# Window attention and a two-layer MLP in split f32: where split weights live, which engine takes the rests, and from which chunk seven products are used

## The chip, the cores and the metric

One NeuronCore of one Trainium2 chip; the other cores are idle. The metric is the device time of one execution in microseconds, median of several runs. A core has five engines with instruction queues of their own: PE (TensorE, matrix products), ACT (ScalarE), DVE (VectorE), POOL (GpSimd) and SP (SyncE, which here issues the DMAs). Each runs its instructions strictly in its order and waits on semaphores where an operand or a room isn't ready.

## The reference

Attention in windows, then a two-layer MLP; everything is f32, and the tokens of all batches are the rows of the MLP.

```python
def _attn_ref(q, k, v):                       # 8 batches, 8 heads, 576 positions, 64 wide
    scores = scale * np.matmul(q, k.transpose(0, 1, 3, 2))
    mask_plain = (rel >= 0) & (rel < window)                                  # window 32
    mask_dil = (rel >= 0) & (rel < window * dilation) & (rel % dilation == 0)  # dilation 4
    masks = [mask_plain if h < H // 2 else mask_dil for h in range(H)]
    scores = np.where(masks, scores, -1000000000.0)
    attn = np.exp(scores - max); attn = attn / (sum(attn) + 1e-09)
    return np.matmul(attn, v)
def _moe_ref(x, w_in, w_out):                 # x 4608 x 512, w_in 512 x 2048, w_out 2048 x 512
    h = x @ w_in
    g = np.where(h > 0.0, h, np.exp(np.minimum(h, 0.0)) - 1.0)
    return (g @ w_out)
```

## The kernel before

**Chunks.** The MLP's 4608 tokens go in nine chunks of 512 (`TC`). In a chunk the hidden width is 16 blocks `f` of 128 (`NF`). `gemm1` makes the block h (128 hidden by 512 tokens), `elu` makes g of it (ACT exp and relu, one DVE instruction, L555 or L557), and `second_product` adds g times w_out into four output banks. GEMM2 of f comes two blocks after GEMM1 of f (`LAG = 2`).

**Split operands.** A product at full f32 accuracy costs PE a doubled pass per product, so operands are split: a high part, rounded to the format PE takes at full pace (ACT, a copy), and a rest, operand minus high part, made by one subtraction (DVE). A product is then three: high·high, high·rest, rest·high. The names are `wh`/`wl` for weights (`split_w`, L180, L181), `xh`/`xl` for tokens (`split_x`, L522), `gh`/`gl` for g (L563, L564). In chunk 0 the first blocks are done before anything is split, with plain f32 products: GEMM1 for f < 7 (`F1`), GEMM2 for f < 11 (`F2`).

**Chunk 0 also turns the weights to f32.** They arrive as 64-bit words (512 KB for a block of 128 x 512). They are taken in 16 pairs k = 0..15, in order of need: pair k holds w_in of block k+1 and w_out of block k−1 (pair 0 holds w_in of 0 and 1, pair 15 w_out of 14 and 15). For each pair ACT takes the magnitude of the upper word (`magnitude`, L129) and DVE makes the f32 bits with four instructions (`convert`): two TENSOR_SCALAR (L137, L139) and two SCALAR_TENSOR_TENSOR (L147, L149). From k = 4 on, two pairs go in one set of 2048 wide instructions. The rooms: raw words in `r0` to `r3` (two pairs each, used in turn), f32 in `a0` to `a7`. In chunk 0 and 1 the split weights take rooms that have come free; the table `LATE` lists where.

**Attention.** Batch 0 runs ahead of the MLP (`first_attention`, and the loads of pairs 1 to 3 come behind its maxima, L112, L115). Batch 1 runs within chunk 0 (`second_attention`): E makes scores, masks, maxima and exponentials; X normalises and transposes on DVE; O multiplies by v. Its exponentials are 12 small ACT instructions that also sum. Later batches run beside later chunks.

**Plain and combined chunks.** Chunks 0 to 2 (`CS = 3`) do GEMM1 block by block. From chunk 3 on it is done in groups of four blocks with seven products of half size in place of eight (`combined_chunk`). These need sums of weight blocks, split again (`combine`: f32 blocks, kept in DRAM by `keep_whole`, come back; four adds, two casts, two rests; stores into the DRAM scratch `combined`). Eight of these are done, three in chunk 1 and five in chunk 2 (`COMBINE`). In a combined chunk the weights come from the scratch through four rooms of `r0`.

**What sets the order.** A scheduler places instructions of each engine by priority; `keep_in_program_order` and `issue_after(x)` tie an instruction to an earlier one of the same engine only. SP takes its DMA issues in one queue.

Of the kernel before, what the change touches and what calls it, by code (L numbers as in the profile page):

```python
# [35 lines left out]
NR = NF // 4  # L36
NE = 2
LAG = 2
F1 = 7
F2 = 11  # L40
# [3 lines left out]
CS = 3  # L44
# [10 lines left out]
WHEN = {1: (0, 6, 7, 13), 2: (1, 6, 7, 12)}  # L55
# [3 lines left out]
PLAIN = ("a5", "a-1'")  # L59
COMBINE = {(1, 11): 0, (1, 13): 1, (1, 15): 2, (2, 1): 3, (2, 4): 4, (2, 6): 5, (2, 9): 6, (2, 11): 7}  # L60
# [6 lines left out]
def body(ctx: ExitStack, tc: tile.TileContext, q, k, v, masks, w_in, w_out, out):  # L67
# [19 lines left out]

    early2 = [wst.tile([P, 2, 4 * DM], F32, name=f"r{NR - NE + i}") for i in range(NE)]
    early = [early2[i // 2][:, i % 2, :] for i in range(2 * NE)]
# [3 lines left out]
    raw2, raw, full4, full2, full = [None] * (NF // 2), [None] * NF, [None] * (NF // 2), [None] * NF, [None] * 2 * NF  # L93
# [12 lines left out]
    def load_w(k, behind=None):  # L106

        if k % 2 == 0:
            raw2[k // 2] = wst.tile([P, 4, DM], I64, name=f"r{k // 2 % NR}")
        raw[k] = raw2[k // 2][:, k % 2 * 2:k % 2 * 2 + 2, :]  # L110
        if behind is not None:
            nc.gpsimd.tensor_copy(out=raw[k].bitcast(F32)[:QB, :, 0:1], in_=behind[:, 0:2].unsqueeze(2))  # L112
        for t in range(2):
            i = need[2 * k + t]
            nc.sync.dma_start(out=raw[k][:, t, :], in_=(w_in, w_out)[i % 2][i // 2])  # L115

    def words(j):

        u = raw2[j].rearrange("p t c -> p (t c)").bitcast(U32).rearrange("p (c two) -> p c two", two=2)
        return u[:, :, 0], u[:, :, 1]  # L120

    def magnitude(k):
        j, part = k // 2, slice(k % 2 * 2 * DM, (k % 2 + 1) * 2 * DM)
        if k % 2 == 0:
            full4[j] = wst.tile([P, 4, DM], F32, name=f"a{j}")
        full2[k] = full4[j][:, k % 2 * 2:k % 2 * 2 + 2, :]
        for t in range(2):
            full[need[2 * k + t]] = full2[k][:, t, :]
        return nc.scalar.activation(out=full4[j].rearrange("p t c -> p (t c)")[:, part], in_=words(j)[1][:, part].bitcast(F32), func=AF.Abs)  # L129

    def convert(j, keep=lambda ins: ins, part=slice(0, 4 * DM), behind=None):

        lo, hi = [u[:, part] for u in words(j)]
        a = full4[j].rearrange("p t c -> p (t c)")[:, part]
        au = a.bitcast(U32)

        keep(nc.vector.tensor_scalar(out=a, in0=a, scalar1=TINY, scalar2=None, op0=ALU.max))  # L137

        keep(nc.vector.tensor_scalar(out=au, in0=au, scalar1=0x07FFFFFF, scalar2=3, op0=ALU.bitwise_and, op1=ALU.logical_shift_left))  # L139
# [12 lines left out]
    taken = {}  # L152

    def room_of(name):

        if name not in taken:
            taken[name] = wst.tile([P, 4 if name[0] == "a" else 8, DM], F32 if name in PLAIN else F32R, name=name[:3].rstrip("'"))
        return taken[name]

    def slots(name, *at):  # L160

        step = at[1] - at[0] if len(at) > 1 else 1
        return room_of(name)[:, at[0]:at[-1] + 1:step, :]
# [12 lines left out]
    def split_w(k, t0, t1, places=None):

        h, l = places or places_of(k, t0, t1)
        w = full2[k][:, t0:t1, :]
        nc.scalar.copy(out=h, in_=w)  # L180
        nc.vector.tensor_tensor(out=l, in0=w, in1=h.bitcast(F32), op=ALU.subtract)  # L181
        for t in range(t0, t1):
            wh[need[2 * k + t]], wl[need[2 * k + t]] = h[:, t - t0, :], l[:, t - t0, :]

    LATE = {0: (("r3", 0, 1), ("r3", 2, 3)), 1: (("r3", 4, 5), ("r3", 6, 7)), 2: (("a7", 0, 1), ("a7", 2, 3)),
# [22 lines left out]
    whole = [tc.dram_tile([P, 2, DM], F32, name=f"whole{p}") for p in range(NF // 2)]  # L208

    def keep_whole(k):  # L210

        for t in range(2):
            i = need[2 * k + t]
            if i % 2 == 0:
                nc.sync.dma_start(out=whole[i // 4][:, i // 2 % 2, :], in_=full[i])

    def combine(p):

        o = p % 2 * 2
# [17 lines left out]
    last_transpose = [None] * B  # L237
# [122 lines left out]
    def exponential(u, sm, nmx, sums):  # L360
        nc.scalar.activation(out=sm[:, u, :], in_=sm[:, u, :], func=AF.Exp, bias=nmx[:, u:u + 1], scale=0.125, accum_out=sums[:, u:u + 1])

# [10 lines left out]
    def exponentials(b, hp, places, sm=None):  # L373
# [8 lines left out]
        nc.vector.tensor_reduce(out=nmx, in_=sm, op=ALU.max, axis=mybir.AxisListType.X)  # L382
        if b == 1:

            maxima.append(nc.vector.tensor_scalar(out=nmx, in0=nmx, scalar1=-0.125, scalar2=None, op0=ALU.mult).ins)
            for u in range(NU):
                exponential(u, sm, nmx, sums)
        else:
            nc.vector.tensor_tensor(out=sm, in0=sm, in1=nmx.unsqueeze(2).broadcast_to([QB, 2 * NU, 2 * G]), op=ALU.subtract)
            nc.scalar.activation(out=sm, in_=sm, func=AF.Exp, scale=0.125)  # L390
            nc.vector.tensor_reduce(out=sums, in_=sm, op=ALU.add, axis=mybir.AxisListType.X)
        return b, hp, sm, nmx, sums

    def probabilities(b, hp, sm, nmx, sums):

        if b == 1:

            for u in range(NU, 2 * NU):
                exponential(u, sm, nmx, sums)
        normalise(nc.vector, sm, sums, lambda ins: ins)  # L400
        tr = transposed()
        for c in range(GU):
            for r in range(2):
                ks, cs, rs = slice((c + r) * G, (c + r + 1) * G), slice(c * G, (c + 1) * G), slice(r * G, (r + 1) * G)
                last_transpose[b] = nc.vector.transpose(out=tr[ks, :, cs], in_=sm[cs, :, rs]).ins
# [24 lines left out]
    def later_probabilities(b, hps, groups):  # L430

        other_sm = slots("a5", 2, 3).rearrange("p o t -> p (o t)")[:QB, :2 * NU * 2 * G].rearrange("p (u j) -> p u j", u=2 * NU)
# [78 lines left out]
    def split_x(c):  # L511
        for hp in range(NC):
# [3 lines left out]
            while t0 < (c + 1) * TC:  # L516
# [5 lines left out]
                last = nc.vector.tensor_tensor(out=xl[hp][:, u], in0=src, in1=xh[hp][:, u].bitcast(F32), op=ALU.subtract)  # L522
# [21 lines left out]
    def elu(h_ps, c, f, v=nc.vector, a=nc.scalar):  # L544
# [16 lines left out]
        gh = slots("r3", 4)[:, 0, :] if (c, f) == (CS - 1, NF - 1) else fp.tile([P, TC], F32R, name="gh", bufs=3)  # L561
        gl = slots("r3", 6)[:, 0, :] if (c, f) == (CS - 1, NF - 2) else slots("a7", 0)[:, 0, :] if (c, f) == (CS - 1, NF - 1) else fp.tile([P, TC], F32R, name="gl", bufs=2)
        high.append(a.copy(out=gh, in_=e).ins)  # L563
        low.append(v.tensor_tensor(out=gl, in0=e, in1=gh.bitcast(F32), op=ALU.subtract).ins)  # L564
# [71 lines left out]
    def take_places():  # L636

        pairs = [tuple(halved(slots(r, o)) for o in at) for r, at in (("a0", (0, 2)), ("a1", (0, 2)), ("r3", (0, 1)))]
# [3 lines left out]
        rows.extend((slots("a-1'", 0, 1), slots("a-1'", 2, 3), slots("a5", 0, 1)))  # L642
        sets.extend(((slots("r1", 0, 1), slots("r1", 2, 3)), (slots("r3", 2, 3), slots("r2", 0, 1)), (slots("a7", 0, 2), slots("a6", 0, 2))))
# [326 lines left out]
```

## Time and profile before

| | us |
|---|---|
| time, median of 3 runs (lowest to highest) | 893.19 (892.83 to 894.97) |
| the profiled execution: time | 892.59 |
| the profiled execution: span in the trace | 890.7 |
| mean granted clock of PE | 0.99 |

The page shows one execution. "busy" is the time in which an engine had an instruction under way; PE's is partly modelled, and a product that waits for its operand can look longer. "x" is a count of instructions, "out<-in" the program's names of tiles, and "<-" behind an idle time what ended it. In the views by stretches, each row has a stretch, its length, busy times of PE, PEld (weight loads), DVE, ACT and POOL, the granted clock, the DMA share and GB/s. In timelines, the first two numbers are start and length.

### The profile page before, as it was taken

The numbers are of one execution on the slowest core, as the hardware profiler recorded it, in microseconds if no ns is written. First come the engines' busy times: TensorE is split into PE (matmuls) and PEld (weight loads), VectorE is DVE, ScalarE is ACT, GpSimd is POOL, SyncE is SP. The second block draws the span as 40 slices with busy tenths as digits, with TensorE's granted clock in tenths as the row PEclk, the third lists the DMA queues.
The fourth block names the chain that finished last, engine by engine and source line by source line (L and its number), as shares of the span: only waits on it lengthen the run. The fifth ranks groups of instructions, "written<-read, shape, count | busy, mean of one in ns | idle before, by whom it ended". The sixth has DMA issues, their size and how long they took to land. (4 is left out here: it accounts for less than half of the span.)

```text
span 890.7 us, 17847 instructions
## 1 busy us (share of the span) xinstructions
PE 866.9 (97%) x7424; PEld 728.4 (82%) x7424; DVE 610.1 (68%) x921; ACT 458.6 (51%) x783; POOL 6.0 (1%) x12
## 2 busy tenths in 40 slices
PE   6999998999989999999999999999999999999998
PEld 4545676887878888898989998989899999998996
DVE  6999996958578878874977487748775533353332
ACT  3665665745655564544554454545554453454334
POOL 2000000000000000000000000000000000000000
PEclk8999998999999999999999999999999999999999
DMA  9996334321463556867576577666765566567541
GB/s 345 380 353 244 118 102 142 109 91 67 160 223 114 192 176 197 255 191 222 179 252 212 182 221 226 220 199 221 212 186 160 175 206 186 171 182 221 185 142 48
DMA packets 66961, 170.68 MB, mean 192 GB/s; under 512 B 6752, under 2 KB 21440, under 8 KB 66880
## 3 DMA queue, kind: packets, MB, share of 16 engines
q1 hardware_dynamic: 66880, 169.54, 59.2%
q8 instruction: 59, 0.97, 0.4%
q14 instruction: 22, 0.18, 0.1%
HBM read 141.20 MB, written 28.31 MB: 190 GB/s over the span
## 5 line engine op out<-in xcount | busy, mean ns | idle before, releaser
L104 PE MATMUL h<-xh,r 128*128 128x256 f32 (+1 forms) x984 | 225.3, 311 | 8.3 <-ACT r L180 3.7
L104 PEld LDWEIGHTS h<-xh,r 128*128 128x128 f32 x984 | 166.2, 192 | 19.9 <-ACT r L180 4.2
L104 PE MATMUL h<-xl,r 128*128 128x256 f32 (+1 forms) x492 | 143.6, 309 | 0.6 <-DVE xl L418 0.6
L104 PE MATMUL o_ps<-a,r 128*128 128x512 f32 x480 | 117.0, 391 | 0.0
L418 DVE SCALAR_TENSOR_TENSOR a-1_3251<-a-1_3251,a 128x1024 f32<-128x1024 f32 x48 | 58.7, 1223 | 83.2 <-ACT a L418 83.0
L418 DVE TENSOR_TENSOR a-1_3251<-h,e 128x512 f32<-128x512 f32 x72 | 49.7, 690 | 82.5 <-PE h L104 82.1
L104 PEld LDWEIGHTS h<-xl,r 128*128 128x128 f32 x492 | 94.4, 192 | 10.4 <-issue 3.5
L104 PEld LDWEIGHTS o_ps<-a,r 128*128 128x128 f32 x480 | 87.6, 188 | 16.5
L104 PE MATMUL o_ps<-a,gh 128*128 128x512 f32 x248 | 89.3, 463 | 0.0
L418 ACT COPY e<-h 128x512 f32<-128x512 f32 x72 | 42.2, 586 | 79.2 <-PE h L104 64.8
L104 PE MATMUL h<-a,r 128*128 128x256 f32 x576 | 77.5, 284 | 0.0
L104 PEld LDWEIGHTS h<-a,r 128*128 128x128 f32 x576 | 74.0, 191 | 3.0
L418 ACT COPY a-1_3251<-h 128x512 f32<-128x512 f32 x24 | 14.1, 587 | 109.6 <-PE h L104 109.6
L104 PEld LDWEIGHTS o_ps<-a,gh 128*128 128x128 f32 x248 | 46.3, 188 | 24.2 <-issue 17.2
L418 ACT ACTIVATE a<-a 128x1024 f32<-128x1024 f32 (+1 forms) x56 | 57.0, 1030 | 1.3
L104 PE MATMUL o_ps<-r,r 128*128 128x512 f32 x212 | 56.8, 391 | 0.0
L104 PE MATMUL o_ps<-a,a 128*128 128x512 f32 x216 | 54.6, 391 | 0.0
L418 ACT ACTIVATE a<-a-1_3251 128x1024 f32<-128x1024 f32 x48 | 51.0, 1062 | 1.3 <-DVE a-1_3251 L418 0.5
L104 PEld LDWEIGHTS o_ps<-a,a 128*128 128x128 f32 x216 | 39.4, 189 | 7.4
L418 ACT CAST r<-a-1_3251 128x1024 fp32r<-128x1024 f32 x32 | 33.6, 1051 | 22.2 <-DVE a-1_3251 L418 22.1
L104 PEld LDWEIGHTS o_ps<-r,r 128*128 128x128 f32 x212 | 38.7, 188 | 7.3
L418 DVE TENSOR_TENSOR r<-a-1_3251,r 128x1024 fp32r<-128x1024 f32 x32 | 39.0, 1218 | 6.6 <-ACT r L418 6.1
(176 smaller groups left out, 1434.0 us busy)
## 6 DMA issues: line engine op xcount, KB each, us to landing
r<-combined SPq DMA_DIRECT2D x168, 512.0 KB, 4.1
vt<-v SPq DMA_DIRECT2D x30, 384.0 KB, 4.3
kt<-k SPq DMA_DIRECT2D x30, 304.0 KB, 4.6
out<-e SPq DMA_DIRECT2D x35, 256.0 KB, 3.3
qt<-q SPq DMA_DIRECT2D x30, 288.0 KB, 3.9
r<-w_in SPq DMA_DIRECT2D x16, 512.0 KB, 7.8
r<-w_out SPq DMA_DIRECT2D x16, 512.0 KB, 7.9
combined<-a SPq DMA_DIRECT2D x20, 256.0 KB, 3.4
```

The source lines that it names most:

```text
L104: return inorder(nc.tensor.matmul(*args, **kw))
L418: return lambda *args, **kw: inorder(getattr(self.eng, name)(*args, **kw))
```

## The change

It does five things.

1. Each pair of weights gets a room of its own, `s0` to `s15`. Once the pair is f32, its high part and rest are written into the room of its 64-bit words. The f32 values go to a room `f` (two in turn; for k < 4 to `s10` and `s11`). All 16 pairs are split in chunk 0 (pairs 0 to 3 at f = 4 to 7, `RESPLIT`), so chunk 1 splits none, and nothing of `keep_whole` is left. Plain f32 products are used for fewer blocks: GEMM1 for f < 5, GEMM2 for f < 3.
2. Pairs are converted one by one, 1024 wide.
3. POOL takes the rests of weights (two instructions of 128 x 512 for a pair), the rests of chunk 0's tokens, the rests of g in chunk 0, and of batch 1 the subtraction of the maximum and the multiplication by 1/sum. One wide exp on ACT takes the place of the 12 small ones, and a DVE reduction sums.
4. `combine` runs on POOL; it makes f32 blocks as `wh` plus `wl`. All eight are in chunk 1.
5. `CS` is 2: chunk 1 is the last plain one, chunk 2 the first with seven products.

```diff
-CS = 3
+CS = 2
-F1 = 7
-F2 = 11
+PLAIN = 4
+F1 = PLAIN + 1
+F2 = PLAIN - 1
-COMBINE = {(1, 11): 0, (1, 13): 1, (1, 15): 2, (2, 1): 3, (2, 4): 4, (2, 6): 5, (2, 9): 6, (2, 11): 7}
+COMBINE = {0: 0, 2: 1, 4: 2, 5: 3, 7: 4, 8: 5, 10: 6, 11: 7}
+RESPLIT = {4: 0, 5: 1, 6: 2, 7: 3}
+LOADS = {0: (8, 9), 1: (12, 13), 3: (14, 15), 5: (10,), 7: (11,)}
...
     def load_w(k, behind=None):
-        if k % 2 == 0:
-            raw2[k // 2] = wst.tile([P, 4, DM], I64, name=f"r{k // 2 % NR}")
+        raw[k] = wst.tile([P, 2, 2 * DM], U32, name=f"s{k}")
...
+    def split_w(k, eng=None):
+        pair[k] = wst.tile([P, 2, 2, DM], F32R, name=f"s{k}")
+        h, l = pair[k][:, :, 0, :], pair[k][:, :, 1, :]
+        nc.scalar.copy(out=h, in_=whole[k])
+        for t in range(2):
+            (eng or nc.gpsimd).tensor_tensor(out=l[:, t, :], in0=whole[k][:, t, :], in1=h[:, t, :].bitcast(F32), op=ALU.subtract)
...
     def combine(p):
-        w = slots("a5", o, o + 1)
-        nc.sync.dma_start(out=w, in_=whole[p])
+        pool = nc.gpsimd
+        for i in range(2):
+            f = 2 * (2 * p + i)
+            pool.tensor_tensor(out=w[:, i, :], in0=wh[f].bitcast(F32), in1=wl[f].bitcast(F32), op=ALU.add)
-        nc.vector.tensor_tensor(out=a22, in0=a21, in1=a22, op=ALU.add)
+        pool.tensor_tensor(out=a22, in0=a21, in1=a22, op=ALU.add)
...
-            for u in range(NU):
-                exponential(u, sm, nmx, sums)
+        (nc.gpsimd if b == 1 else nc.vector).tensor_tensor(out=sm, in0=sm, in1=nmx.unsqueeze(2).broadcast_to([QB, 2 * NU, 2 * G]), op=ALU.subtract)
+        nc.scalar.activation(out=sm, in_=sm, func=AF.Exp, scale=0.125)
+        nc.vector.tensor_reduce(out=sums, in_=sm, op=ALU.add, axis=mybir.AxisListType.X)
...
-        normalise(nc.vector, sm, sums, lambda ins: ins)
+        normalise(nc.gpsimd if b == 1 else nc.vector, sm, sums, lambda ins: ins)
...
-        low.append(v.tensor_tensor(out=gl, in0=e, in1=gh.bitcast(F32), op=ALU.subtract).ins)
+        low.append((nc.gpsimd if c == 0 else v).tensor_tensor(out=gl, in0=e, in1=gh.bitcast(F32), op=ALU.subtract).ins)
...
-    for j in range(2 * (NR - NE), 2 * NR + 2):
+    for j in range(4, 8):
         load_w(j)
...
-                    split_x(0)
+                    split_x(0, nc.gpsimd)
...
-            if c == 0 and F1 <= f + 2 <= NF:
+            if c == 0 and PLAIN <= f + 1 < NF:
                 with tc.issue_after(hidden[-2]):
-                    split_w(f + 1, 0, 2 if f >= F2 else 1)
+                    split_w(f + 1)
+            if c == 0 and f in RESPLIT:
+                with tc.issue_after(hidden[-1]):
+                    split_w(RESPLIT[f])
```

The order of instructions moves at three places that matter in what follows. A row is line, operation, output and inputs.

First place, SP's queue just ahead of chunk 0. Before, behind two pairs of `qt` and `kt` (attention's loads), pair 1 (`r_117`), then pairs 2 and 3 (`r_261`):

```order
L253 DMA qt<-q 128x576
L254 DMA kt<-k 128x608
L253 DMA qt<-q 128x576
L254 DMA kt<-k 128x608
L115 DMA r_117<-w_in 128x512
L115 DMA r_117<-w_out 128x512
L115 DMA r_261<-w_in 128x512
L115 DMA r_261<-w_out 128x512
L115 DMA r_261<-w_in 128x512
L115 DMA r_261<-w_out 128x512
```

After, from the second half of pair 4 (`s_502`) on; `s_505` to `s_519` are pairs 5 to 9, `s_204` is pair 1:

```order
L112 DMA s_502<-w_out 128x1024
L112 DMA s_505<-w_in 128x1024
L112 DMA s_505<-w_out 128x1024
L112 DMA s_508<-w_in 128x1024
L112 DMA s_508<-w_out 128x1024
L112 DMA s_511<-w_in 128x1024
L112 DMA s_511<-w_out 128x1024
L112 DMA s_516<-w_in 128x1024
L112 DMA s_516<-w_out 128x1024
L112 DMA s_519<-w_in 128x1024
L112 DMA s_204<-w_in 128x1024
L112 DMA s_204<-w_out 128x1024
```

Pair 1 has moved from behind the attention's loads to behind pairs 4 to 8 and half of pair 9, eleven halves with the first of pair 4. Pair 2 and pair 3 follow further down, behind the other half of pair 9 and pair 14.

ACT at the first blocks of chunk 0, before (`a_337`, `a_521` are the f32 of pairs 0/1 and 2/3, `e` and `h` those of the ELU):

```order
L286 COPY x_122<-b 128x288 x2
L129 ACTIVATE a_337<-r_117 128x1024
L129 ACTIVATE a_521<-r_261 128x1024 x2
L550 ACTIVATE e<-h_465 128x512
L552 ACTIVATE e<-e 128x512
L550 ACTIVATE e<-h_544 128x512
L552 ACTIVATE e<-e 128x512
```

And after, with `s_204`, `s_256`, `s_335` the words of pairs 1, 2, 3:

```order
L127 ACTIVATE s_332<-s_204 128x1024
L127 ACTIVATE s_514<-s_256 128x1024
L516 ACTIVATE e<-h_461 128x512
L518 ACTIVATE e<-e 128x512
L127 ACTIVATE s_514<-s_335 128x1024
L516 ACTIVATE e<-h_544 128x512
```

The magnitude of pair 2 stands ahead of the first block's exp as before, while that of pair 3 has moved behind it.

Second place, DVE in the middle of chunk 0, before. `a_725` and `a_817` are the f32 of pairs 6/7 and 8/9, `sm` the softmax of batch 1, `pt` its transpose:

```order
L147 SCALAR_TENSOR_TENSOR a_725<-r_511,a_725 128x2048
L149 SCALAR_TENSOR_TENSOR a_725<-r_511,a_725 128x2048
L137 TENSOR_SCALAR a_817<-a_817 128x2048
L298 TENSOR_SCALAR sums<-sums 96x12
L139 TENSOR_SCALAR a_817<-a_817 128x2048
L299 RECIPROCAL sums<-sums 96x12
L181 TENSOR_TENSOR a-1_792<-a_725,a-1_792 128x512 x2
L147 SCALAR_TENSOR_TENSOR a_817<-r_516,a_817 128x2048
L300 TENSOR_TENSOR sm<-sm,sums 96x768
L555 SCALAR_TENSOR_TENSOR gh<-h_824,e 128x512
L149 SCALAR_TENSOR_TENSOR a_817<-r_516,a_817 128x2048
L405 STREAM_TRANSPOSE pt_79<-sm 32x12x32 x6
```

DVE after, in the same part (`s_511` and `s_516` are pairs 7 and 8, `f` their f32):

```order
L523 SCALAR_TENSOR_TENSOR e<-h_789,e 128x512
L359 TENSOR_REDUCE sums<-sm 96x12
L138 TENSOR_SCALAR f<-f 128x1024
L273 TENSOR_SCALAR sums<-sums 96x12
L146 SCALAR_TENSOR_TENSOR f<-s_511,f 128x1024
L274 RECIPROCAL sums<-sums 96x12
L148 SCALAR_TENSOR_TENSOR f<-s_511,f 128x1024
L136 TENSOR_SCALAR f<-f 128x1024
L138 TENSOR_SCALAR f<-f 128x1024
L369 STREAM_TRANSPOSE pt_79<-sm 32x12x32 x6
L146 SCALAR_TENSOR_TENSOR f<-s_516,f 128x1024
L523 SCALAR_TENSOR_TENSOR e<-h_854,e 128x512
```

And POOL after, where nothing stood before (`s_810`, `s_875`, `s_925` are the split pairs 6, 7, 8):

```order
L531 TENSOR_TENSOR gl<-e,gh 128x512
L357 TENSOR_TENSOR sm<-sm,nmx 96x768
L159 TENSOR_TENSOR s_810<-f,s_810 128x512 x2
L531 TENSOR_TENSOR gl<-e,gh 128x512
L275 TENSOR_TENSOR sm<-sm,sums 96x768
L159 TENSOR_TENSOR s_875<-f,s_875 128x512 x2
L531 TENSOR_TENSOR gl<-e,gh 128x512
L159 TENSOR_TENSOR s_925<-f,s_925 128x512 x2
```

Rests and the multiplication have left DVE's row; a reduction has come; the conversions are half as wide and twice as many. POOL has a rest of g and two rests of weights for each block.

Third place, DVE at the end of chunk 0, before, from the last conversion (`a_1126`, pairs 14/15) on:

```order
L149 SCALAR_TENSOR_TENSOR a_1126<-r_732,a_1126 128x2048
L298 TENSOR_SCALAR sums<-sums 96x12
L299 RECIPROCAL sums<-sums 96x12
L557 SCALAR_TENSOR_TENSOR e<-h_1175,e 128x512
L300 TENSOR_TENSOR sm<-sm,sums 96x768
L181 TENSOR_TENSOR r_1196<-a_1126,r_1196 128x2x512
L405 STREAM_TRANSPOSE pt_79<-sm 32x12x32 x6
L181 TENSOR_TENSOR r_1196<-a_1126,r_1196 128x2x512
L564 TENSOR_TENSOR gl<-e,gh 128x512
L557 SCALAR_TENSOR_TENSOR e<-h_1211,e 128x512
L564 TENSOR_TENSOR gl<-e,gh 128x512
L522 TENSOR_TENSOR xl_1316<-x_122,xh_1315 128x64
```

And after (`s_649` is pair 15):

```order
L146 SCALAR_TENSOR_TENSOR f<-s_649,f 128x1024
L369 STREAM_TRANSPOSE pt_79<-sm 32x12x32 x6
L523 SCALAR_TENSOR_TENSOR e<-h_1308,e 128x512
L148 SCALAR_TENSOR_TENSOR f<-s_649,f 128x1024
L523 SCALAR_TENSOR_TENSOR e<-h_1345,e 128x512
L488 TENSOR_TENSOR xl_1452<-x_116,xh_1451 128x64
L488 TENSOR_TENSOR xl_1452<-x_532,xh_1451 128x448
L488 TENSOR_TENSOR xl_1458<-x_116,xh_1457 128x64
L488 TENSOR_TENSOR xl_1458<-x_532,xh_1457 128x448
L488 TENSOR_TENSOR xl_1464<-x_116,xh_1463 128x64
```

The multiplication, the rests of weights and the rests of g behind the last conversion are gone from DVE, and the transposes stand ahead of it.

More of the change, by code (lines that the diff above doesn't have):

```diff
@@ L35 @@
 AHEAD = 3
-NR = NF // 4
-NE = 2
 LAG = 2
-F1 = 7
-F2 = 11
+PLAIN = 4
+F1 = PLAIN + 1
+F2 = PLAIN - 1
 NEG = -1.0e9
@@ L833, in body @@
     for c in range(CS):
-        if c == 1:
-            with tc.issue_after(hidden[-4]), tc.issue_after(below[-4]):
-                last_x = split_x(c)
-        elif c > 1:
+        if c > 0:
             split_x(c)
-        if c == 1:
-            for j in (14, 15, 12, 13, *range(12)):
-                keep_whole(j)
         when = WHEN.get(c, ())
```

176 lines of the change are left out of this document (70 added, 106 removed), and 3 rows, old and new, of the table LATE.

## The prediction

> **What bounds the kernel now.** First the page: busy shares, and the span in 40 slices of 22.3 us.
>
> ```profile
> PE 866.9 (97%) x7424; PEld 728.4 (82%) x7424; DVE 610.1 (68%) x921; ACT 458.6 (51%) x783; POOL 6.0 (1%) x12
> PE   6999998999989999999999999999999999999998
> DVE  6999996958578878874977487748775533353332
> ```
>
> PE is busy nearly everywhere, but DVE's row says that slices 2 to 6 are of another kind: nines, then six to eight. So the next view is the busy time by stretches, cut where I saw chunk 0 begin (28.4) and chunk 1 begin (139.5); after the length and the five engines stand clock, DMA share and GB/s.
>
> ```profile
> 28.40:60.00 31.60, 31.25 (x235) 14.62 (x234) 30.11 (x41) 20.86 (x49) 0.00 (x0) 1.00 1.01 377
> 60.00:100.00 40.00, 39.82 (x228) 22.73 (x227) 39.68 (x51) 23.76 (x75) 0.00 (x0) 1.00 0.66 226
> 100.00:139.50 39.50, 35.59 (x240) 24.47 (x238) 37.39 (x51) 25.14 (x62) 0.00 (x0) 0.99 0.29 94
> ```
>
> Chunk 0 takes 111.1 us, and DVE is busy for 30.11 + 39.68 + 37.39 = 107.2 of them (neighbouring records overlap a little). PE looks as full, but a product that waits for its operand stretches there, and every product of f needs what DVE converted just before. DVE paces chunk 0; PE paces the rest. In the first stretch the DMA share is 1.01: the loads are at their limit too, 377 GB/s.
>
> At the seam to chunk 1 the timeline of PE, and of DVE at its last conversion:
>
> ```profile
> 139.49 0.80 PE L104 MATMUL h<-xh,r 128*128 128x512 f32 x1 [3.75 <-ACT r L180]
> 121.80 2.28 DVE L149 SCALAR_TENSOR_TENSOR a<-r,a 128x2048 uint32<-128x2048 uint32 x1
> ```
>
> DVE ends its last conversion at 124.1; chunk 1 starts 15.4 us later, and PE's last wait there (3.75 us) is for the split of pair 0.
>
> **The change, part by part.** Each sum is made against the profiled 892.6 us (span 890.7 and 1.9 around it), 0.6 below the median of 893.2, which is less than the 0.3% (2.7 us) that a measurement of this kernel can tell from no change.
>
> *Combined chunks.* The stretches of chunks 1 to 5, cut at their first GEMM1 products:
>
> ```profile
> 139.50:240.00 100.50, 99.14 (x769) 81.07 (x770) 72.21 (x122) 57.47 (x103) 0.00 (x0) 0.97 0.37 122
> 240.00:338.00 98.00, 95.39 (x896) 78.24 (x895) 77.19 (x145) 54.97 (x100) 0.00 (x0) 0.98 0.52 167
> 338.00:429.00 91.00, 89.37 (x897) 80.29 (x896) 67.12 (x102) 43.16 (x66) 0.00 (x0) 1.00 0.70 218
> 429.00:522.00 93.00, 93.00 (x917) 83.78 (x916) 67.19 (x103) 45.65 (x66) 0.00 (x0) 1.00 0.68 214
> ```
>
> Now chunk 1 is the last plain one (98.0, as chunk 2 was), chunk 2 the first with seven products (91.0), chunk 3 a later one (93.0). Chunks 1 to 3 took 100.5 + 98.0 + 91.0 = 289.5 and should take 282.0: **−7.5**. If a PE pause of chunk 2 goes with it, for which the waits name nobody, it is about 2.4 more:
>
> ```profile
> PE h L104 <- issue: 2.4, 1, 2.4
> ```
>
> *DVE's own work up to the last conversion.* Mean durations, grouped by shape within chunk 0:
>
> ```profile
> L149 DVE SCALAR_TENSOR_TENSOR a<-r,a 128x2048 uint32<-128x2048 uint32 x6 | 13.7, 2286 | 0.1
> L147 DVE SCALAR_TENSOR_TENSOR a<-r,a 128x2048 uint32<-128x2048 uint32 x6 | 13.7, 2281 | 0.0
> L405 DVE STREAM_TRANSPOSE pt<-sm 32x384 f32<-32x384 f32 x24 | 13.6, 567 | 0.3
> L555 DVE SCALAR_TENSOR_TENSOR gh<-h,e 128x512 f32<-128x512 f32 x11 | 7.5, 680 | 0.1
> L139 DVE TENSOR_SCALAR a<-a 128x2048 uint32<-128x2048 uint32 x6 | 7.3, 1221 | 0.0
> L137 DVE TENSOR_SCALAR a<-a 128x2048 f32<-128x2048 f32 x6 | 7.3, 1219 | 0.0
> L181 DVE TENSOR_TENSOR r<-a,r 128x1024 fp32r<-128x1024 f32 x5 | 6.0, 1218 | 0.3 <-ACT r L180 0.3
> L369 DVE TENSOR_TENSOR sm<-a_ps,masks_sb 96x384 f32<-96x384 f32 x8 | 4.0, 544 | 0.0
> L300 DVE TENSOR_TENSOR sm<-sm,sums 96x768 f32<-96x768 f32 x4 | 3.8, 948 | 0.0
> L382 DVE TENSOR_REDUCE nmx<-sm 96x12 f32<-96x768 f32 x4 | 3.8, 942 | 0.0
> L149 DVE SCALAR_TENSOR_TENSOR a<-r,a 128x1024 uint32<-128x1024 uint32 x3 | 3.7, 1227 | 0.2
> L564 DVE TENSOR_TENSOR gl<-e,gh 128x512 fp32r<-128x512 f32 x5 | 3.4, 686 | 0.8 <-ACT gh L563 0.8
> L522 DVE TENSOR_TENSOR xl<-x,xh 128x448 fp32r<-128x448 f32 x4 | 2.5, 617 | 0.0
> L137 DVE TENSOR_SCALAR a<-a 128x1024 f32<-128x1024 f32 x3 | 2.1, 693 | 0.8 <-ACT a L129 0.8
> L522 DVE TENSOR_TENSOR xl<-x,xh 128x64 fp32r<-128x64 f32 x4 | 0.9, 218 | 0.0
> ```
>
> Ahead of the last conversion leave DVE: six narrow rests of weights (0.69 each, half the wide one or a little over) and two wide (1.22), four rests of x (0.69), two of gl (0.69), three multiplies (0.95), four small negations (0.2): 6.6 + 2.8 + 1.4 + 2.8 + 0.7 = 14.3. Come: four sums (0.94) 3.8; the fourth set of six transposes (0.57) and its small steps, moved ahead of it, 3.8; one ELU step 0.7; and twelve pairs converted 1024 wide instead of six times two, 12 x (2 x 0.69 + 2 x 1.22) − 6 x (2 x 1.22 + 2 x 2.28) = 45.8 − 42.0 = 3.8. Sum **−2.2**.
>
> *After the last conversion.* Before, DVE still had a multiply, four wide rests, six transposes, three gl, three ELU steps and the rests of x of chunk 1, and PE then waited for pair 0. Now only two ELU steps and the rests of x (4 x (0.62 + 0.22) = 3.4) are left, 4.8, of which not all runs ahead of chunk 1: 15.4 becomes some 6 with ACT's casts between. **−9.4**. PE's own saving (fewer doubled fp32 products) stays hidden, since it isn't the pace here.
>
> *Later loads.* Pair 1 is issued at 14.52 and 15.77, pair 3 last, and what follows is DVE's conversion of pair 1 and PE's product for f=2:
>
> ```profile
> 14.52 0.33 SPq L115 DMA_DIRECT2D r<-w_in  x1
> 21.16 0.43 SPq L115 DMA_DIRECT2D r<-w_out  x1
> r<-w_out SPq DMA_DIRECT2D x16, 512.0 KB, 7.9
> 32.17 3.25 ACT L129 ACTIVATE a<-r 128x1024 f32<-128x1024 f32 x3
> 36.15 1.23 DVE L149 SCALAR_TENSOR_TENSOR a<-r,a 128x1024 uint32<-128x1024 uint32 x1
> 38.15 3.27 PE L104 MATMUL h<-x,a 128*128 128x512 f32 x7 [0.35 <-DVE gh L555]
> ```
>
> With 7.9 us to landing pair 1 is there by about 23.7, pair 3 by 29.1. Now eleven halves of pairs 4 to 9 stand ahead of pair 1 in SP's queue and one qt/kt pair less: at 377 GB/s a half (524 KB) takes 1.39, so +15.3 − 1.6 = +13.7: about 37.4. Pair 2 follows near 43, pair 3 near 48. ACT's order makes it worse: the magnitude of pair 2 stands ahead of the first ELU's exp, and DVE's order has that ELU step ahead of the last instruction of pair 1. So pair 1 is ready at 43 + 1.1 (magnitude) + 1.2 (exp, relu) + 0.7 + 1.2 = 47 instead of 37.4. Pair 3's conversion ends near 58 instead of 48.4. DVE has no idle time later in which to catch up: **+9.5**. Bounds: 0 if the queue in truth hands out in another order, +11.
>
> *POOL's work beside DVE.* This is the large one, and the profile shows the pair at one place only, DVE and POOL at 16.7 to 21:
>
> ```profile
> 16.69 0.17 DVE L298 TENSOR_SCALAR sums<-sums 96x12 f32<-96x12 f32 x1
> 17.27 1.47 POOL L300 TENSOR_TENSOR r<-r,sums 96x768 f32<-96x768 f32 x1 [2.22 <-ACT pt L355]
> 17.96 0.80 DVE L298 TENSOR_SCALAR sums<-sums 96x12 f32<-96x12 f32 x1
> 19.17 1.47 POOL L300 TENSOR_TENSOR r<-r,sums 96x768 f32<-96x768 f32 x1 [0.43 <-DVE sums L299]
> 19.87 0.95 DVE L331 TENSOR_TENSOR r<-b,nmx 96x768 f32<-96x768 f32 x1
> ```
>
> The same TENSOR_SCALAR took 0.17 us alone and 0.80 beside POOL, and ended at 18.76, when POOL did (18.74): it was held up. The TENSOR_TENSOR at 19.87, which reads one operand from PSUM, was not. No row shows a DVE instruction with two SBUF operands beside POOL: the conversions' SCALAR_TENSOR_TENSOR and, in chunk 1, gl. By SBUF words moved in and out they are nearer to the held form: 3.0 per ns for a TENSOR_SCALAR (1024 in, 1024 out in 0.69), 2.5 for them (2048 in, 1024 out in 1.22), 0.8 for the free one, which only writes there. I take them as held. The Trainium skill, SBUF — State Buffer, § Who interferes with whom, has the same as a rule: a DVE instruction with two SBUF inputs contends with a GpSimd one that reads SBUF, the pair is taken for the whole instruction, and the other is blocked. The trace agrees for the TENSOR_SCALAR (0.17 to 0.80); for two SBUF inputs it has no case.
>
> How long POOL works: 768 wide in 1.47, so 512 wide about 1.0 (by proportion, with a small fixed part). From where DVE becomes busy for good to the last conversion POOL has 10 pairs of weight rests, 10 rests of gl and 7 softmax steps: 20 x 1.0 + 10 x 1.0 + 7 x 1.47 = 41. Of DVE's 96 us in that time the ELU steps, mask sums, reductions and transposes (14 x 0.69 + 8 x 0.54 + 8 x 0.94 + 24 x 0.57 = 35) would go on, the rest would wait. W is what DVE waits: 0 at one end, 41 at the other; if everything fell in the free work 41 − 35 = 6; by chance 41 x 61/96 = 26. I take **+25**. The softmax steps now also go DVE, POOL, ACT, DVE; between its two ends DVE has 4 to 7 us of other work, which covers POOL's 1.5 and ACT's 0.9 but no queue on POOL (0 to +5, taken in the range).
>
> *Chunk 1.* All eight weight sums, on POOL 8 x (4 x 1.0 + 4 x 0.6, a 256-wide step with the fixed part) = about 52 us, run beside PE-paced work, where DVE is busy 72.2 of 100.5 and products lag two f behind: **+2.5**, 0 to +12.
>
> Sum: 892.6 − 7.5 − 2.2 − 9.4 + 9.5 + 25 + 2.5 = 910.5, with the median's 0.6 some **911**.
>
> **The rivals.** *POOL and DVE mostly pass one another*, the other side: only TENSOR_SCALARs are held, or POOL's work falls beside DVE's free work. Without W the sum is 886.1, so W under 4.4 makes the kernel faster by more than 0.3% (886 to 890), and W of 4.4 to 9.8 leaves it within (to 895.9). For it: one free case stands beside the held one. Against it: conversions are three fifths of DVE's 96 us (15 pairs at 3.8), and POOL's 41 us can't find 35 us of free work by chance. *The late loads are caught up*: 901. Against it: DVE leaves under 2 us idle in the first two stretches and 2.1 in the third. *POOL's sums are late for chunk 2*: DVE makes the first operand of chunk 2 in a room that POOL's last sums have to leave, in program order ahead of the ELU step of f=13. If the 52 us, themselves held up by DVE, run past f=12 of chunk 1 (some 75 us after its start), the ELU steps wait and PE with them: +8 to +12, 919 to 923.
>
> **How the numbers follow.** Forecast (W from 15 to 33, 901 to 919): 0.44. Sums late, or the softmax steps queued on POOL, above 919: 0.10. W from 10 to 15, 896 to 901: 0.06. W from 4.4 to 10, or 15 with the loads caught up: 0.10, within 0.3% (890.5 to 895.9). Below that 0.30: the bound W = 0, some of it with late loads that cost less or PE's pause of 2.4 gone, so down to 882. Faster 0.30, same 0.10, slower 0.44 + 0.10 + 0.06 = 0.60. With 0.05 left out on either side the range is 882 to 921.
>
> **What would show it.** ACT's exp of f=0 near 44 and PE idle from about 38 to 47 (late loads). Means of L136, L138, L146, L148 above 0.69 and 1.22, with POOL's instructions ending where theirs end (the wait). Chunk 1 starting near 163 instead of 139.5, only 6 us after the last conversion; chunk 2 near 91. I am wrong if these means stay at 0.69 and 1.22, or if chunk 1 starts before 145.

## The result, and the profile after

| | us |
|---|---|
| after, median of 4 runs (lowest to highest) | 938.81 (933.96 to 941.8) |
| before, median of 4 runs beside them | 893.74 (892.83 to 894.97) |
| ratio, 95% interval | 1.0498 (1.0446 to 1.055) |
| the profiled execution after: time, span | 941.8, 940.0 |

The change made the kernel slower by 5%. The forecast was 911, so about 2%: the sign held, the size didn't. The profiled execution is the longest of the four. From its page, the busy row and the tenths of DVE and POOL (a slice is 23.5 us):

```profile
PE 869.6 (93%) x7608; PEld 743.8 (79%) x7608; DVE 638.4 (68%) x867; ACT 445.8 (47%) x662; POOL 176.5 (19%) x133
DVE  6599999867877875977597659765966453354322
POOL 2175668777940000000000000000000000000000
```

DVE is nearly full over the first slices, and POOL's work stands beside it in the same slices. Next the busy times by stretches, cut at the end of DVE's last conversion (176.5), at the first GEMM1 product of chunk 1 (184.2), and at the starts of chunks 2, 3 and 4 (columns as before):

```profile
28.40:176.50 148.10, 106.96 (x692) 70.05 (x692) 136.41 (x132) 63.46 (x89) 91.97 (x56) 0.88 0.43 154
176.50:184.20 7.70, 7.70 (x48) 6.01 (x47) 4.95 (x7) 5.72 (x14) 7.62 (x7) 0.82 0.16 52
184.20:289.90 105.70, 95.58 (x896) 76.72 (x895) 76.11 (x111) 54.83 (x94) 70.89 (x60) 1.00 0.47 153
289.90:381.00 91.10, 89.73 (x899) 80.53 (x898) 67.39 (x106) 43.18 (x67) 0.00 (x0) 1.00 0.71 221
381.00:474.00 93.00, 92.65 (x915) 83.40 (x914) 67.08 (x101) 45.52 (x67) 0.00 (x0) 1.00 0.68 213
```

Against the stretches of before, this is where the profiled 49.3 us of span went:

| stretch | before | after | moved | forecast |
|---|---|---|---|---|
| chunk 0 to the end of the last conversion | 28.4 to 124.1 | 28.4 to 176.5 | +52.4 | +9.5 − 2.2 + 25 = +32.3 |
| from there to chunk 1 | 15.4 | 7.7 | −7.7 | −9.4 |
| chunks 1 to 3 | 289.5 | 105.7 + 91.1 + 93.0 = 289.8 | +0.3 | −7.5 + 2.5 = −5.0 |
| chunk 4 to the end | 461.7 | 466.0 | +4.3 | 0 |

PE's granted clock is 0.88 in chunk 0, where it was 1.00 before. That can explain little of the longer chunk 0, since from 51.7 us on DVE is busy for 123.33 of 124.80 us and hardly waits for anybody:

```profile
51.70:176.50 124.80, 91.79 (x571) 63.00 (x570) 123.33 (x112) 53.46 (x75) 87.48 (x53) 0.89 0.32 107
```

The conversions of pairs 4 to 15 on DVE, and POOL's rests for the same pairs, grouped by shape (the view runs from 28.4 to 180):

```profile
L146 DVE SCALAR_TENSOR_TENSOR f<-s,f 128x1024 uint32<-128x1024 uint32 x12 | 24.0, 2004 | 0.3
L148 DVE SCALAR_TENSOR_TENSOR f<-s,f 128x1024 uint32<-128x1024 uint32 x12 | 22.1, 1838 | 0.2
L136 DVE TENSOR_SCALAR f<-f 128x1024 f32<-128x1024 f32 x12 | 19.4, 1614 | 0.4 <-ACT f L127 0.4
L138 DVE TENSOR_SCALAR f<-f 128x1024 uint32<-128x1024 uint32 x12 | 14.1, 1173 | 0.1
L138 DVE TENSOR_SCALAR s<-s 128x1024 uint32<-128x1024 uint32 x3 | 8.9, 2961 | 0.1
L369 DVE STREAM_TRANSPOSE pt<-sm 32x384 f32<-32x384 f32 x24 | 13.6, 568 | 0.3
L523 DVE SCALAR_TENSOR_TENSOR e<-h,e 128x512 f32<-128x512 f32 x12 | 8.1, 678 | 0.1
...
L159 POOL TENSOR_TENSOR s<-f,s 128x512 fp32r<-128x512 f32 x24 | 37.0, 1562 | 12.9 <-ACT s L157 12.8
```

At this width the conversion instructions took 0.69 and 1.22 us before; now their means are 1.2 to 2.0. The transposes (568 ns) and the ELU step (678 ns) are what they were. For each form, take what its instructions last beyond the shortest of them, and call the sum the held time: from 28.4 to the last conversion it is 47 us, 27.6 in TENSOR_SCALARs and 19.0 in SCALAR_TENSOR_TENSORs; before it was 2.

### The profile page after: what moved, and what is told of

It is laid out like the page before. It is cut to its first block, busy times and chain, and to the rows that moved or that the text cites. A ratio compares the mean times of both kernels' runs of the same rounds, so it can differ in the third digit from the quotient of the medians.

```text
span 940.0 us, 18197 instructions
## 1 busy us (share of the span) xinstructions
PE 869.6 (93%) x7608; PEld 743.8 (79%) x7608; DVE 638.4 (68%) x867; ACT 445.8 (47%) x662; POOL 176.5 (19%) x133
## 5 line engine op out<-in xcount | busy, mean ns | idle before, releaser
L103 PE MATMUL o_ps<-s,s 128*128 128x512 f32 x1276 | 317.5, 391 | 0.0
L103 PE MATMUL h<-xh,s 128*128 128x256 f32 (+1 forms) x1112 | 250.8, 308 | 26.4 <-DVE e L523 17.8
L103 PEld LDWEIGHTS o_ps<-s,s 128*128 128x128 f32 x1276 | 233.1, 188 | 44.2
L103 PEld LDWEIGHTS h<-xh,s 128*128 128x128 f32 x1112 | 187.8, 192 | 43.5 <-DVE e L523 15.9
L103 PE MATMUL h<-xl,s 128*128 128x256 f32 (+1 forms) x556 | 162.3, 309 | 1.7 <-issue 0.7
L103 PE MATMUL h<-s,s 128*128 128x256 f32 x1008 | 136.3, 285 | 1.8 <-ACT e L382 1.8
L103 PEld LDWEIGHTS h<-s,s 128*128 128x128 f32 x1008 | 129.5, 191 | 8.0 <-ACT e L382 2.2
L382 DVE SCALAR_TENSOR_TENSOR s<-s,f 128x1024 f32<-128x1024 f32 x56 | 68.5, 1223 | 92.8 <-ACT f L382 92.7
L103 PEld LDWEIGHTS h<-xl,s 128*128 128x128 f32 x556 | 107.6, 194 | 9.1 <-DVE xl L382 0.9
L103 PE MATMUL o_ps<-s,gh 128*128 128x512 f32 x248 | 83.3, 423 | 0.7 <-POOL s L159 0.7
L382 DVE TENSOR_TENSOR s<-s,s 128x1024 fp32r<-128x1024 f32 x56 | 68.2, 1217 | 13.4 <-ACT s L382 12.7
```

The lines of the kernel that those rows point to most:

```text
L103: return inorder(nc.tensor.matmul(*args, **kw))
L382: return lambda *args, **kw: inorder(getattr(self.eng, name)(*args, **kw))
```

## The experiments

Times are medians, each beside the kernel before on its chip (893.0 to 894.2). The changed kernel's own four runs lie between 934.0 and 941.8, so a difference of less than some 4 us against it is not clear of the scatter.

**Is it POOL that holds DVE, and which forms?** The first run is a kernel of streams alone. Its core, with `vec` one of seven DVE forms (two more streams have POOL's fills in place of its subtractions):

```diff
+    for vec in (ts, stt, tt, elu, reduce, transpose, ts_strided):
+        phase(vec, 6, nothing, 0)
+        phase(vec, 6, pool, 8)
```

> Not the kernel's computation: only streams of single instructions, six on DVE, alone and then beside eight POOL subtractions of 128 x 512 (two SBUF operands); the output is filler. If the theory holds (POOL holds what DVE needs for a second SBUF operand and for the fast TENSOR_SCALAR), beside POOL the TENSOR_SCALAR 128x1024 grows from 0.69 us to several us (in the changed kernel one took 7.50, through six POOL instructions in a row), the SCALAR_TENSOR_TENSOR 128x1024 from 1.22 to about 2.2 to 2.5, and the subtraction of two SBUF operands from 0.69 to about 1.7; the ELU form with one operand from PSUM (0.68), the reduction and the transpose don't grow. The strided TENSOR_SCALAR is open: longer alone, and if only the fast form is held, unchanged beside POOL. POOL's fills write only: SCALAR_TENSOR_TENSOR beside them shouldn't grow. The rival (conversions are slow in the changed kernel for another reason, such as the room or the DMA beside them) expects no growth in any stream.

DVE's timeline there, six instructions a row. TENSOR_SCALAR and SCALAR_TENSOR_TENSOR stand first alone, then beside POOL's subtractions. The next three rows are beside subtractions too: two operands from SBUF (L107), the ELU form (L110), the strided TENSOR_SCALAR (L101). The last two are beside POOL's fills:

```profile
12.44 4.34 DVE L98 TENSOR_SCALAR a<-a 128x1024 f32<-128x1024 f32 x6 [12.44 <-ACT a L133]
17.56 10.11 DVE L98 TENSOR_SCALAR a<-a 128x1024 f32<-128x1024 f32 x6 [0.78 <-ACT a L133]
30.47 7.52 DVE L104 SCALAR_TENSOR_TENSOR a<-words,a 128x1024 uint32<-128x1024 uint32 x6 [2.81 <-ACT a L133]
38.77 12.24 DVE L104 SCALAR_TENSOR_TENSOR a<-words,a 128x1024 uint32<-128x1024 uint32 x6 [0.78 <-ACT a L133]
60.26 9.03 DVE L107 TENSOR_TENSOR d<-d,a 128x512 f32<-128x512 f32 x6 [0.78 <-ACT a L133]
78.64 4.32 DVE L110 SCALAR_TENSOR_TENSOR d<-h_ps,a 128x512 f32<-128x512 f32 x6 [0.88 <-ACT a L133]
129.42 9.04 DVE L101 TENSOR_SCALAR a<-words 128x1024 f32<-128x1024 f32 x6 [0.78 <-ACT a L133]
153.56 6.04 DVE L98 TENSOR_SCALAR a<-a 128x1024 f32<-128x1024 f32 x6 [15.09 <-ACT a L133]
160.99 7.53 DVE L104 SCALAR_TENSOR_TENSOR a<-words,a 128x1024 uint32<-128x1024 uint32 x6 [1.40 <-ACT a L133]
```

The theory holds: TENSOR_SCALAR goes from 4.34 to 10.11 for six, SCALAR_TENSOR_TENSOR from 7.52 to 12.24, the subtraction of two SBUF operands to 9.03 (4.32 alone); the ELU form with PSUM stays at 4.32, and so do the reduction (7.49) and the transpose (3.57). Beside POOL's fills, which only write, SCALAR_TENSOR_TENSOR is not held (7.53), while TENSOR_SCALAR is a little (6.04). The Trainium skill, SBUF — State Buffer, § Who interferes with whom, states that a DVE instruction with two SBUF inputs contends with a GpSimd instruction that reads SBUF and not with one that only writes it, that `tensor_scalar` can contend through its two-port modes, and that an instruction with at most one SBUF input outside these modes does not. This run agrees with each. Seen one by one, DVE and POOL take turns: a pair lasts 1.67 us with TENSOR_SCALAR and 2.20 with SCALAR_TENSOR_TENSOR. A turn costs DVE about 0.95 (1.63 for 0.69, 2.17 for 1.22), and POOL's subtraction, 1.26 alone, lasts 1.59 and 2.12.

The same question in the kernel, with POOL's work of chunk 0 put back on DVE:

```diff
-            (eng or nc.gpsimd).tensor_tensor(out=l[:, t, :], ...
+            nc.vector.tensor_tensor(out=l[:, t, :], ...
-        low.append((nc.gpsimd if c == 0 else v).tensor_tensor(
+        low.append(v.tensor_tensor(
-                    split_x(0, nc.gpsimd)
+                    split_x(0)
-        (nc.gpsimd if b == 1 else nc.vector).tensor_tensor(out=sm, ...
+        nc.vector.tensor_tensor(out=sm, ...
-        normalise(nc.gpsimd if b == 1 else nc.vector, sm, sums, ...
+        normalise(nc.vector, sm, sums, ...
```

> The changed kernel with all of POOL's work of chunk 0 back on DVE (rests of weights, of x, of g, both softmax steps); the weight sums of chunk 1 stay on POOL. Theory: DVE loses its 46 us of held time up to the last conversion and gets 36 us of work, so about 10 us less: 929, with L136/L138 at 0.69 and L146/L148 at 1.22 in chunk 0. Rival (conversions are slow for another reason than POOL): means stay near 1.6 and 2.0 and 36 us come on top: 975.

It took 929.8, with these means:

```profile
L146 DVE SCALAR_TENSOR_TENSOR f<-s,f 128x1024 uint32<-128x1024 uint32 x12 | 15.7, 1306 | 0.0
L148 DVE SCALAR_TENSOR_TENSOR f<-s,f 128x1024 uint32<-128x1024 uint32 x12 | 14.6, 1217 | 0.1
L138 DVE TENSOR_SCALAR f<-f 128x1024 uint32<-128x1024 uint32 x12 | 8.2, 686 | 0.1
L136 DVE TENSOR_SCALAR f<-f 128x1024 f32<-128x1024 f32 x12 | 8.2, 686 | 0.0
```

The means are back at 0.69 and 1.22, but for L146: eleven of its twelve take 1.22, and the last, beside POOL's first weight sum, 2.31. The rival (975) is out: this work costs DVE less when DVE does it than when POOL does it beside DVE. Two further runs make one half of the edit each:

> The changed kernel with only the 32 rests of weights back on DVE. Theory: POOL keeps about 33 of its 74 us of chunk 0; DVE gets 22 us and loses some 25 of its 46 held: 933 to 941, no large change. Rival (another reason): +22, 961.

It took 936.8, within the range and not clear of the changed kernel's scatter.

> The changed kernel with the rests of g and x of chunk 0 and both softmax steps back on DVE, the rests of weights still on POOL. Theory: DVE gets 19 us of work and loses some 20 of its 46 held: 934 to 942. Rival (another reason): +19, 958.

It took 930.2, 4 us below the range I gave. Moving the rests of weights alone hardly changes the time; moving the small steps does. The trace of the changed kernel shows a reason at the place where a TENSOR_SCALAR lasted longest. DVE's timeline and POOL's:

```profile
54.50 0.67 DVE L521 SCALAR_TENSOR_TENSOR gh<-h,e 128x512 f32<-128x512 f32 x1
55.10 7.50 DVE L138 TENSOR_SCALAR s<-s 128x1024 uint32<-128x1024 uint32 x1
62.63 2.17 DVE L146 SCALAR_TENSOR_TENSOR s<-s,s 128x1024 uint32<-128x1024 uint32 x1
...
53.98 1.92 POOL L357 TENSOR_TENSOR sm<-sm,nmx 96x768 f32<-96x768 f32 x1
55.87 4.95 POOL L488 TENSOR_TENSOR xl<-x,xh 128x512 fp32r<-128x512 f32 x4
60.78 2.93 POOL L159 TENSOR_TENSOR s<-s,s 128x512 fp32r<-128x512 f32 x2
```

That is no turn: DVE waited through the softmax step, four rests of x and a rest of weights. Five more holds, of 3.4 to 4.5 us, begin in a softmax step as well. The first idea was that POOL keeps DVE out for as long as its instructions don't wait for one another.

```diff
-        ko(nc.gpsimd.tensor_tensor(out=z, in0=x, in1=y, op=ALU.subtract))
+        ko(nc.gpsimd.tensor_tensor(out=zs[turn[0]], in0=x, in1=y, op=ALU.subtract))
```

> Only streams again (output is filler): six DVE instructions beside eight POOL subtractions, first with POOL's instructions independent of one another, so that it takes them without a pause, then with each waiting for the one before (as in the first streams, where DVE and POOL took turns, 1.67 us for a pair with TENSOR_SCALAR and 2.20 with SCALAR_TENSOR_TENSOR). Theory (POOL keeps the ports for as long as it runs without a pause): the first held TENSOR_SCALAR beside the independent ones lasts until the eighth has ended, about 10 us, the others 0.69; SCALAR_TENSOR_TENSOR likewise, 10 to 11 us once; with the chained ones they take turns again, 1.63 and 2.17. Rival (turns always, and the 7.50 us in the changed kernel has another cause): 1.63 and 2.17 each time. The ELU form with PSUM stays at 0.69 in both.

DVE's six TENSOR_SCALARs beside independent subtractions, then beside chained ones:

```profile
42.72 10.09 DVE L99 TENSOR_SCALAR a<-a 128x1024 f32<-128x1024 f32 x6 [42.72 <-ACT a L135]
94.40 10.11 DVE L99 TENSOR_SCALAR a<-a 128x1024 f32<-128x1024 f32 x6 [5.80 <-ACT a L135]
```

This idea fell: they take turns both times. The second idea was the softmax step's shape:

```diff
+    for parts, shared in ((96, True), (96, False), (128, True), (128, False)):
+        one(parts, shared, ts)        # POOL: 768 wide on `parts`, then four of 128x512
+        one(parts, shared, stt)
```

> Only streams (output is filler): POOL takes a step of 768 elements and then four subtractions of 128x512; DVE takes the ELU form (0.69, not held) and then three TENSOR_SCALARs or three SCALAR_TENSOR_TENSORs. The step is, in turn, 96 x 768 with the operand that a softmax step has (12 values, each read 64 times), 96 x 768 with a full operand, the same two with 128 partitions; a last stream is the first with chained subtractions. In the changed kernel the six longest holds (3.4 to 7.5 us, through two to six POOL instructions) all began while POOL was in a softmax step with more work queued behind it. Theory: such a step lets POOL keep the ports for what follows, so a held instruction there lasts 5 us or more; the four shapes say whether the 96 partitions or the repeated operand do it. Rival (turns are always taken, and those holds have another cause): no DVE instruction is held through more than one POOL instruction, at most 2.2 for TENSOR_SCALAR and 2.7 for SCALAR_TENSOR_TENSOR.

Three TENSOR_SCALARs on DVE's timeline: behind a step of 96 partitions with the repeated operand, with a full one, and behind 128 partitions with the repeated operand:

```profile
35.03 7.30 DVE L106 TENSOR_SCALAR a<-a 128x1024 f32<-128x1024 f32 x3
...
54.59 7.63 DVE L106 TENSOR_SCALAR a<-a 128x1024 f32<-128x1024 f32 x3
...
74.64 4.58 DVE L106 TENSOR_SCALAR a<-a 128x1024 f32<-128x1024 f32 x3
```

The first of each three took 4.90, 5.23 and 1.25. With 96 partitions, whatever the second operand, DVE got in only after three of the four subtractions behind; with 128 it took its turn, and with 96 and chained subtractions as well (1.31). So of the cases run, it takes both: a step of 96 partitions, and subtractions queued behind it that don't wait. In the kernel, the same order on POOL with 128 partitions:

```diff
-            sm = ap.tile([QB, 2 * NU, 2 * G], F32, name="sm", bufs=1)
+            sm = ap.tile([P if b == 1 else QB, 2 * NU, 2 * G], F32, name="sm", bufs=1)
...
+            nc.gpsimd.tensor_tensor(out=sm1, in0=sm1, in1=nmx1.unsqueeze(2).broadcast_to([P, 2 * NU, 2 * G]), op=ALU.subtract)
```

> The changed kernel with POOL's eight softmax steps on 128 partitions in place of 96 (the 32 further rows are filled by ACT and not used); POOL's order and amount of instructions are the same. Theory (behind a step of 96 partitions POOL lets no held DVE instruction in until it has done what is queued behind): the six longest holds shrink to one turn, 7.50 + 3.38 + 4.44 + 4.46 + 4.40 + 4.32 = 28.5 against 4 x 1.7 + 2 x 2.2 = 11.2, so 17 us less: 921 to 923. Rival (the six long holds only gather waits that would fall elsewhere): 935 to 939.

It took 927.3, 11.5 less, where 16 to 18 were expected. The TENSOR_SCALAR of 7.50 now reads

```profile
55.93 1.36 DVE L138 TENSOR_SCALAR s<-s 128x1024 uint32<-128x1024 uint32 x1
```

and no conversion lasts over 2.4 us any more. DVE's held time of chunk 0 is 34 us in place of 47: 12 of the 17 came back, and 5 fell elsewhere.

> The changed kernel with only batch 1's softmax steps back on DVE; rests of weights, x and g stay on POOL. Theory: the six long holds go (17 us), eight further turns of POOL go (some 7 us), and DVE gets 8 x 0.95 = 7.6 us: 921 to 924. Rival (the six gather waits that would fall elsewhere): some 938.

It took 931.5, 7 less, where 15 to 18 were expected. The long holds are gone, but four of DVE's eight new TENSOR_TENSORs are themselves held (2.04 us in place of 0.94, 4.4 in all), which I had left out. The held time is 34 us here too, so 13 less, and 7.6 us of work came to DVE: that makes 5 less, and the last conversion ends 5.2 earlier (171.3). Both runs say the same of the mechanism; the sizes expected were too high.

**Are the late loads an item of their own?**

```diff
     for j in range(4, 8):
-        load_w(j)
+        with tc.issue_after(loads[-1]):
+            load_w(j)
```

> The changed kernel with the loads of pairs 4 and up issued behind those of pairs 1 to 3; nothing else. Theory (late loads are an item of their own): 9 us less, 930, with pair 1 converted by 38 and not 46. Rival (what DVE and POOL do to one another hides it): 939, no change.

It took 933.0, 6 less. GEMM1 of f=2 starts at 41.2 (46.1 in the changed kernel, 38.2 before). A part of the 9 went to the first long hold, which starts earlier and lasts 9.32 here, 1.8 more.

> Both together: POOL's work of chunk 0 back on DVE, and the loads in order; the weight sums stay on POOL. If the two are separate items of the sum, 929.8 less 9: 921. If they cover the same time, 928 to 930.

It took 917.1, 4 below the sum of two separate items: with chunk 0's work on DVE the loads are worth 12.7.

> The softmax steps on 128 partitions, and the loads in order as well. If both are items of their own: 17 for the long holds and the 6 that the loads in order gave alone: 915 to 917.

It took 924.0, so the loads gave 3.3 on top. In both runs where POOL still holds DVE they are worth less than 12.7. Why isn't settled: here the last conversion ends 5.8 earlier than without the loads in order (159.6 for 165.4), but chunk 2 starts only 2.0 earlier (274.1 for 276.1).

> The variant with chunk 0's work on DVE and the loads in order (917.1), and batch 1's softmax as before the change: 12 small exponentials on ACT that also sum, so DVE has no subtraction and no sums. Theory (DVE paces chunk 0, so each us of its work there is a us of time): 4 x (0.95 + 0.94 − 0.17) = 6.9 us less, 910. Rival (chunk 0 is no longer DVE's pace in this variant): 917.

It took 915.4, only 1.7 less. The last conversion ends 2.9 earlier (154.6 for 157.5), yet chunk 2 starts 2.2 later (267.5 for 265.3): what DVE saved in chunk 0 was lost again by then. What took it wasn't followed up.

**Chunk 1 and the number of plain chunks.** What PE waited for in the changed kernel from 184 to 290 (us in total, times, longest):

```profile
PE h L103 <- ACT h L514: 6.4, 4, 2.9
PE h L103 <- ACT nothing L441: 3.4, 3, 1.7
```

In the longest of these waits ACT's copy of h stood behind an exponential that waited for DVE's softmax step (1.47 us there, held; 0.95 alone), and so PE waited.

```diff
-        pool = nc.gpsimd
+        pool = nc.vector
```

> The changed kernel with the weight sums of chunk 1 on DVE, everything else as changed. Theory (in chunk 1, too, POOL's holds cost, 104 us instead of the 98 of the last plain chunk before): up to 6 less, 933. Rival (PE's pace hides DVE's waits there, and 35 us of sums make DVE the bound): 940 to 950.

It took 938.3, no change. Chunk 1 takes 104.7 us; DVE is no longer held there, but has the sums (89.0 us busy, 76.1 in the changed kernel).

> The changed kernel without the arithmetic of the weight sums in chunk 1: the split blocks themselves are stored in place of S2 and S3, so the chunks with seven products use other weights; loads and stores are as many. Theory (the sums cost chunk 1, whichever engine has them: through POOL's holds, or as DVE's own work): chunk 1 falls from 105.7 us to the 98 of the last plain chunk before, 931. Rival (chunk 1 is longer for another reason): 938, no change.

It took 926.3, 12.5 less. This edit leaves out ACT's casts of the sums as well. Chunk 1 by the windows of this run:

```profile
181.00:275.80 94.80, 93.69 (x895) 77.09 (x894) 59.65 (x106) 47.71 (x86) 1.28 (x1) 1.00 0.26 81
```

It takes 94.8 in place of 105.7, so the sums with their casts cost chunk 1 some 11 us, and with DVE in POOL's place about as much (104.7).

> The changed kernel with chunk 2 plain again (three plain chunks, the weight sums in chunk 2, seven products from chunk 3 on); everything else as changed. Theory (chunk 2 with seven products saves time, but less than the 7.5 us of the forecast, as the sums cost the last plain chunk): chunk 1 without sums 98 to 100, chunk 2 with them 105, chunk 3 91, against 105.7 + 91.1 + 93.0: 4 to 6 us more, 943 to 945. Rival (no gain in it): 938.

It took 942.1, 3.3 more, just under the range and within the scatter. Its chunks 1, 2 and 3:

```profile
185.60:281.40 95.80, 95.80 (x770) 78.81 (x770) 57.86 (x102) 48.64 (x89) 1.29 (x1) 1.00 0.17 54
281.40:386.20 104.80, 95.49 (x895) 76.70 (x894) 78.73 (x109) 55.58 (x96) 70.10 (x58) 1.00 0.48 154
386.20:477.30 91.10, 89.70 (x898) 80.51 (x897) 67.14 (x102) 43.16 (x66) 0.00 (x0) 1.00 0.71 221
```

The three take 291.7 where the changed kernel's take 289.8, 1.9 more. So by stretches and by medians seven products in chunk 2 gain about 2 to 3 us, where the forecast had 7.5 for it.

No run beats the kernel before; the fastest variant was 915.4. Spreading the rests of weights back into chunk 1, as before, wasn't tried: their rooms are used again by then.

## Why the prediction was right or wrong

**Right: what paces chunk 0, and the kind of the loss.** DVE paced it, the conversions were held by POOL, and the ELU steps, reductions and transposes were not; the rival "POOL and DVE mostly pass one another" is out. Up to the last conversion the three terms can be read from DVE's busy time. The held time rose from 2 to 47: +45, forecast +25. DVE's own work without it went from 91.77 (93.75 − 1.98) to 89.53 (136.41 − 46.88): −2.2, forecast −2.2. DVE's idle time went from 1.95 to 11.7: +9.7, where +9.5 was forecast for the late loads. Together that is the +52 of the table, and of the 31 us by which the profiled span missed the sum, 20 are W.

**Wrong: the size of W**, "I take +25", and its upper bound of 41. Measured: 45 (47 less the 2 of before). Two steps failed. First, the count of POOL's work: I took it from where "DVE becomes busy for good", 37 instructions, and left its first ones to DVE's idle time. The stretch has 56; the rests of pairs 0 to 3, those of x and the first weight sums ran beside conversions too. A POOL instruction of 128x512 took 1.26 alone, where I had 1.0. So POOL's work was, by an estimate from these times, some 72 us and not 41. Second, the forecast tacitly let a held instruction wait for one POOL instruction. Six holds through two to six POOL instructions are 28.5 us in place of 11.2 by turns. The run with 128 partitions separates the two: without the long holds 34 us are held, and 56 turns of 0.95 at the forecast's share of 61/96 are 34 as well; the long holds add 12 or 13, which gives 47. That 72 us times 61/96, by the forecast's own rule, would come to 46 is luck: a turn costs DVE 0.95 and not 1.26, and the long holds make up the difference. The sum itself had a slip that changed nothing: 20 + 10 + 10.3 is 40.3 and not 41. And the free TENSOR_TENSOR from PSUM does read SBUF as well, twelve values of `nmx`.

**Right: the late loads.** ACT's exp of f=0, and PE's product of f=2 behind its wait:

```profile
42.96 0.59 ACT L516 ACTIVATE e<-h 128x512 f32<-128x512 f32 x1
...
46.12 5.41 PE L103 MATMUL h<-x,s 128*128 128x512 f32 x8 [6.44 <-DVE s L148]
```

They start at 43 and 46, where 44 and 47 were forecast; f=2 starts 8.0 later than before (38.15). What the loads are worth in time depends on the rest: 3.3, 6 and 12.7 us in the three pairs of runs above. **Right: the end of chunk 0**, 7.7 us from the last conversion to chunk 1, where 6 were forecast.

**Right in sign, mis-sized: chunk 1.** Chunks 2 and 3 take 91.1 and 93.0, as forecast. Chunk 1 was to take 98.0 + 2.5 and takes 105.7. The 98.0 came from a plain chunk that already had five sums in it; without any, one takes 94.8 to 95.8, and the eight sums cost 11, at the upper end of the forecast's 0 to +12. So chunks 1 to 3 came out at +0.3 and not −5.0. The rival "sums late for chunk 2" didn't cost anything: POOL's last sum ends at 275.2, 91 us into chunk 1, but DVE makes the first operand of chunk 2 at 277.1, and none of DVE's waits in chunk 1 names POOL.

**Open:** the 4.3 us from chunk 4 on. The profiled executions of the variants vary there as well (463 to 467 us), so no cause is claimed.

## What to carry to other kernels

Work that is moved from a full DVE to an idle POOL isn't hidden where DVE runs TENSOR_SCALARs or instructions with two SBUF operands: a POOL subtraction of 128x512 cost such a DVE 0.95 us in held time, more than the 0.69 that DVE needs to do it itself. Count all of POOL's instructions against the stretch in which they will really run, and look at what stands behind each in POOL's queue. And before spending DVE's gaps, see in which order the DMA queue has the first loads: one that nobody asked for cost 3 to 13 us here.

## What the runs showed of the hardware that was not expected

Beside POOL's subtractions of 128 partitions, independent or chained, DVE and POOL take strict turns (1.67 and 2.20 us a pair). After a POOL instruction of 96 partitions with more queued behind it and no wait between, DVE is let in only several instructions later: the first held instruction lasted 4.9 to 5.8 us behind 96x768 steps, where steps of 128 partitions gave 1.3 to 2.1. Other sizes weren't run, and why 96 partitions do this stays open. A TENSOR_SCALAR that reads every second word is as fast as a dense one (0.69) and is held alike (9.04 us for six), and POOL's fills hold a TENSOR_SCALAR (6.04 for six in place of 4.34) but not a SCALAR_TENSOR_TENSOR.
